# Layer 2's first product of blocks 1 to 4 by seven half-size products, with weights' sums formed during block 0

## The chip, the core and the metric

The kernel runs on one core of a Trainium2 chip. The core has a matrix engine (TensorE, PE in the profile; its weight loads are listed as PEld), a vector engine (VectorE, DVE), a scalar engine (ScalarE, ACT), GpSimd (POOL) and SyncE (SP), which here starts the transfers. Each engine works through its own list of instructions in order; semaphores make one engine wait for another. The matrix engine writes its results to PSUM, which has 8 banks; everything else that is kept on the core lies in SBUF, in tiles of 128 partitions.

The metric is the time of one execution in microseconds (us) on the device. The kernel before took 992.25 us, the median of 3 runs (991.37 to 992.49).

## What is computed

The reference is a causal attention with a memory term, followed by two layers with one hidden product each:

```python
x = attn_out.transpose(0, 2, 1, 3).reshape(B * S, H * D)    # 2304 tokens x 512
# layer 1: h = x @ w_in (512 x 2048); g = softplus(h); x = g @ w_out (2048 x 512)
# layer 2:
h = x @ w_in
r = np.maximum(h, 0.0)
g = r * r
return (g @ w_out).astype(np.float32)
```

B is 4, H is 8, S is 576, D is 64. The weights come as 64-bit floats and are turned into pairs on the core.

## The kernel before

Every matrix product works on pairs of 16-bit numbers: a value is kept as a high half and a low half (what the high half leaves over), and a product is three matmuls: high weights by high data, high weights by low data, low weights by high data (lines 708 to 710).

The kernel first runs attention and layer 1 interleaved, about 618 us of the span. Layer 1 works in 9 blocks of 256 tokens; each ends in `evac_x` (lines 472 to 475), where ScalarE writes the high half of the block's output (scaled by 2) and VectorE the low half (line 475). These halves are the input of layer 2, in tiles `x` of 512 tokens.

Layer 2 (lines 698 to 732) works in blocks of 512 tokens, four of them and a last one of 256, numbered 0 to 4. A block has two stages:

- The first product. For each of 16 chunks `f` of 128 hidden columns, 12 matmuls (4 chunks of the 512 inputs, 3 matmuls each) with 512 moving columns (256 in block 4) fill one PSUM bank `h2ps`. ScalarE applies Relu (712) into `r2` and squares it (713); VectorE makes the high half by a cast (715) and the low half by a subtraction (716). These go to `gg`, one pair of tiles for each `f`.
- The row tiles, one for each 128 tokens: 48 matmuls of 512 columns (724 to 726) sum over all 16 `f` into one bank `ops`; ScalarE copies it to `osb` (728) and SyncE sends it out (731).

`split_piece` (409 to 424) turns pieces of the 64-bit weights into pairs: VectorE has four instructions a piece (419, 420, 421, 424) and ScalarE one (423). Layer 2's 32 pieces go through it late in layer 1 and during block 0's first product: `W3` is w_in, `W4` is w_out.

The order of instructions on each engine is set when the program is built: a list scheduler places them by an estimate of its own, in the order of the code where priorities (`tc.high_priority`) don't say otherwise. The pools set when a tile's memory can be written again.

Of the kernel before, what the change touches and what calls it, by code (L numbers as in the profile page):

```python
# [31 lines left out]
LOE = 99  # L32
TQ = 2
TP = 2
GPL = 0
W34P = 0

KVB = 9
SPB = 2
# [9 lines left out]
def kernel(  # L49
# [15 lines left out]
    pe, act, dve, pool, sp = nc.tensor, nc.scalar, nc.vector, nc.gpsimd, nc.sync  # L65
# [3 lines left out]
    NCC = DM // P  # L69
# [291 lines left out]
    def x_at(kb):  # L361
        i, o = divmod(kb * NB, XB)
        return x_t[i][:, :, o:o + NB]
# [42 lines left out]
            )  # L406
        return t

    def split_piece(i, t, Ws, pool_, on_pool=False):
# [49 lines left out]
    def unit_x(kb, cp, f0=0, f1=NFC):  # L459
# [134 lines left out]
    def run_unit(u):  # L594
        if u[0] == "h":
            unit_h(u[1], u[2])
        elif u[0] == "x":
            unit_x(*u[1:])
        elif u[0] == "xq":
            unit_xq(u[1], u[2])  # L600
        elif u[0] == "close":
            close_start()
        else:
            i = u[1]
            with tc.high_priority(HW):
                split_piece(order[i], pieces.pop(i), (W1, W2), stage, on_pool=False)
# [66 lines left out]
    st2 = ctx.enter_context(st2_cm)  # L673
    nu = len(queue)
    pieces = {i: load_piece(i, (moe2_w_in, moe2_w_out), sp, st2) for i in range(ST2)}
    nxt = 0
# [18 lines left out]
    bp = ctx.enter_context(tc.tile_pool(name="bp", bufs=2, side="right", reuse_waits="tile"))  # L695
    mm2 = ctx.enter_context(tc.tile_pool(name="mm2", bufs=8, space=PSUM, reuse_waits="tile"))
    u2 = S_R / S_X2
    t0 = 0
    while t0 < NT:
        n = min(512, NT - t0)  # L700
        gs = []
        x = x_t[t0 // XB]
        for f in range(NFC):
            ps = mm2.tile([P, 512], F32, tag="mm2", name="h2ps")
            for c in range(NCC):
                wh, wl = (w[:, c, f * P:(f + 1) * P] for w in W3)
                xh, xl = (x[:, t * NCC + c] for t in range(2))
                pe.matmul(ps[:, :n], wh, xh, start=(c == 0), stop=False)  # L708
                pe.matmul(ps[:, :n], wh, xl, start=False, stop=False)  # L709
                pe.matmul(ps[:, :n], wl, xh, start=False, stop=(c == NCC - 1))  # L710
            r = bp.tile([P, 512], F32, name="r2", bufs=3)
            act.activation(r[:, :n], ps[:, :n], AF.Relu, scale=u2)  # L712
            act.activation(r[:, :n], r[:, :n], AF.Square)  # L713
            g = [bp.tile([P, 512], F16, name=f"gg{t}_{f}", bufs=1) for t in range(2)]
            dve.tensor_copy(g[0][:, :n], r[:, :n])  # L715
            dve.tensor_tensor(g[1][:, :n], r[:, :n], g[0][:, :n], ALU.subtract)
            gs.append(g)
            if t0 == 0:
                w34_to(NPC + f + 1)
        for m in range(n // P):  # L720
            ps = mm2.tile([P, 512], F32, tag="mm2", name="ops")
            for f in range(NFC):
                gh, gl = (t[:, m * P:(m + 1) * P] for t in gs[f])
                pe.matmul(ps, gh, W4[0][:, f, :], start=(f == 0), stop=False)  # L724
                pe.matmul(ps, gh, W4[1][:, f, :], start=False, stop=False)  # L725
                pe.matmul(ps, gl, W4[0][:, f, :], start=False, stop=(f == NFC - 1))  # L726
            o = bp.tile([P, 512], F32, name="osb", bufs=3)
            act.activation(o, ps, AF.Copy, scale=1.0 / (S_R * S_R))  # L728
            for b, s0, r0, k_ in segs(t0 // P + m):
                p0 = b * S + s0  # L730
                sp.dma_start(out=out[p0:p0 + k_, :], in_=o[r0:r0 + k_])
        t0 += n


# [27 lines left out]
```

## Time and profile before

| | |
|---|---|
| median of 3 runs | 992.25 us |
| the profiled execution, its own time | 997.09 us |
| its span, first to last instruction | 995.3 us |
| matmul busy | 907.6 us (91%) |
| VectorE busy | 584.9 us (59%) |
| ScalarE busy | 543.2 us (55%) |
| mean granted clock of TensorE | 0.984 of 2.4 GHz |

Busy times are sums of durations as the profiler reports them. A matmul's duration includes its way through the array, and matmuls overlap; the pace of a run of matmuls is read from the starts of its first and last one. A few per cent of the matmul records are missing from the trace, so counts of matmuls in a stretch are slightly low.

### The profile page before, as it was taken

The page shows a single profiled execution, that of the slowest core. Times are in us where ns is not written, and L with a number is a line of the kernel's source. Part 1 is how long each engine was busy: PE and PEld are TensorE (multiplying, and loading weights), DVE is VectorE, ACT ScalarE, POOL GpSimd, SP SyncE. Part 2 cuts the span into 40 slices and gives each one's busy share as a digit, 9 for nine tenths or more (in the row PEclk, how much of TensorE's full clock was granted, in tenths as well). Part 3 has the DMA queues.
Part 4 walks back from the last instruction along what each step waited for, and adds up shares of the span by engine and source line. Part 5 has one row for each costly group of instructions (what it writes and reads, how often), then busy time and mean ns, then how long its engine had stood idle before and what let it go on. Part 6 is the DMA issues. An engine that isn't in the chain of part 4 may idle for free.

```text
span 995.3 us, 20666 instructions
## 1 busy us (share of the span) xinstructions
PE 907.6 (91%) x8418; PEld 642.2 (65%) x8436; DVE 584.9 (59%) x1359; ACT 543.2 (55%) x1090; POOL 2.2 (0%) x10
## 2 busy tenths in 40 slices
PE   4336998899998999999999998999999999999998
PEld 3235787788887889888887886444444444444483
DVE  7998989868668676757755599950340141042040
ACT  8765868769669595958756384630340241142050
POOL 0000000000000000000000000000000000000000
PEclk9998999999999999999998999999999999999999
DMA  9999998775699955756743556500000000000000
GB/s 228 233 232 229 205 174 162 119 105 112 100 169 174 160 102 96 108 97 96 115 84 58 157 178 190 174 14 22 11 1 22 22 1 11 32 1 11 22 13 22
DMA packets 283216, 101.00 MB, mean 101 GB/s; under 512 B 248048, under 2 KB 280816, under 8 KB 283120
## 3 DMA queue, kind: packets, MB, share of 16 engines
q1 hardware_dynamic: 282880, 99.65, 50.5%
q8 instruction: 66, 1.08, 0.5%
q14 instruction: 30, 0.25, 0.1%
q10 hardware_dynamic: 240, 0.02, 0.0%
HBM read 48.78 MB, written 4.72 MB: 54 GB/s over the span
## 4 chain that ended last, share of the span: by engine, by line
PE 67%; DMA 14%; DVE 9%; ACT 5%; issue 3%; SPq 1%; ACTq 0%; DVEq 0%
PE ops L726 7%; DMA PT<-p 6%; PE h2ps L710 6%; PE h2ps L709 6%; PE h2ps L708 6%; PE ops L724 6%; PE ops L725 6%; PE xps L454 4%; PE xps L455 4%; PE xps L453 4%; PE s_ps L311 3%; PE hps L438 3%; PE hps L437 3%; PE hps L436 3%; PE pvt L356 3%
## 5 line engine op out<-in xcount | busy, mean ns | idle before, releaser
L715 DVE CAST gg<-r 128x512 f16<-128x512 f32 (+1 forms) x80 | 31.8, 398 | 238.0 <-ACT r L713 238.0
L436 PE MATMUL hps<-x,W 128*128 128x256 f16 x576 | 160.1, 278 | 3.5 <-DVE cc L275 2.1
L438 PE MATMUL hps<-x,W 128*128 128x256 f16 x576 | 160.0, 278 | 0.0
L437 PE MATMUL hps<-x,W 128*128 128x256 f16 x576 | 160.0, 278 | 0.0
L454 PE MATMUL xps<-g,W 128*128 128x256 f16 x512 | 139.7, 275 | 2.2 <-DVE g L447 2.2
L455 PE MATMUL xps<-g,W 128*128 128x256 f16 x512 | 140.0, 275 | 0.0
L453 PE MATMUL xps<-g,W 128*128 128x256 f16 x512 | 138.6, 275 | 1.3 <-DVE spa L443 0.7
L320 ACT ACTIVATE Pt<-Pt,cs 128x128 f32<-128x128 f32 (+4 forms) x144 | 84.1, 584 | 67.8 <-DVE cs L316 67.5
L311 PE MATMUL s_ps<-KT,qT 128*128 128x128 f16 (+2 forms) x992 | 83.8, 225 | 35.9 <-DVE cs L316 35.3
L708 PE MATMUL h2ps<-x,W 128*128 128x512 f16 (+1 forms) x320 | 114.5, 358 | 0.0
L709 PE MATMUL h2ps<-x,W 128*128 128x512 f16 (+1 forms) x320 | 114.5, 358 | 0.0
L710 PE MATMUL h2ps<-x,W 128*128 128x512 f16 (+1 forms) x320 | 114.5, 358 | 0.0
L726 PE MATMUL ops<-W,gg 128*128 128x512 f16 x288 | 109.2, 379 | 0.9
L724 PE MATMUL ops<-W,gg 128*128 128x512 f16 x288 | 109.2, 379 | 0.0
L728 ACT ACTIVATE osb<-ops 128x512 f32<-128x512 f32 x18 | 10.8, 597 | 172.8 <-PE ops L726 172.8
L725 PE MATMUL ops<-W,gg 128*128 128x512 bf16 x270 | 102.3, 379 | 0.0
L311 PEld LDWEIGHTS <-qT 128*128 128x128 f16 (+1 forms) x992 | 59.2, 105 | 47.7 <-issue 43.1
L333 DVE TENSOR_TENSOR p<-Pt,p 128x512 f16<-128x512 f32 (+2 forms) x104 | 69.5, 668 | 29.1 <-ACT p L332 28.4
L712 ACT ACTIVATE r<-h2ps 128x512 f32<-128x512 f32 (+1 forms) x80 | 44.2, 552 | 75.0 <-PE h2ps L710 75.0
L356 PE MATMUL pvt<-V,PT 128*128 128x64 f16 (+1 forms) x1392 | 62.1, 199 | 16.7 <-DMA PT<-p 15.6
L316 DVE CUSTOM_DVE_ANT_0 Pt<-s_ps,mask 128x128 f32<-128x128 f32 (+3 forms) x128 | 62.1, 485 | 17.3 <-PE s_ps L311 16.8
L332 ACT ACTIVATE p<-Pt 128x512 f16<-128x512 f32 (+2 forms) x104 | 62.9, 605 | 11.3 <-DMA PT<-p 10.3
(117 smaller groups left out, 1648.2 us busy)
## 6 DMA issues: line engine op xcount, KB each, us to landing
wst<-in_moe_w_in_dram SPq DMA_DIRECT2D x32, 512.0 KB, 5.0
wst<-in_moe_w_out_dram SPq DMA_DIRECT2D x32, 512.0 KB, 4.4
rawk<-in_k_dram SPq DMA_DIRECT2D x16, 256.0 KB, 4.1
rawq<-in_q_dram SPq DMA_DIRECT2D x16, 256.0 KB, 3.5
rawv<-in_v_dram SPq DMA_DIRECT2D x16, 256.0 KB, 4.1
out_dram<-osb SPq DMA_DIRECT2D x16, 256.0 KB, 2.0
PT<-p SPq DMA_TRANSPOSE x100, 3.4
mraw<-in_M_prev_dram SPq DMA_DIRECT2D x8, 128.0 KB, 3.8
```

The source lines that it names most:

```text
L311: pe.matmul(o[x * n:(x + 1) * n], qT[g][:, t * H + h, x * n:(x + 1) * n], KT[kb][:, h, a - j * P:e - j * P], start=(t == 0), stop=(t == 1),)
L436: pe.matmul(o, wh, x[:, c], start=(c == 0), stop=False)
L437: pe.matmul(o, wh, x[:, NCC + c], start=False, stop=False)
L438: pe.matmul(o, wl, x[:, c], start=False, stop=(c == NCC - 1))
L453: pe.matmul(ps, wh, gh, start=(f == f0), stop=False)
L454: pe.matmul(ps, wh, gl, start=False, stop=False)
L455: pe.matmul(ps, wl, gh, start=False, stop=(f == f1 - 1))
L708: pe.matmul(ps[:, :n], wh, xh, start=(c == 0), stop=False)
L709: pe.matmul(ps[:, :n], wh, xl, start=False, stop=False)
L710: pe.matmul(ps[:, :n], wl, xh, start=False, stop=(c == NCC - 1))
L724: pe.matmul(ps, gh, W4[0][:, f, :], start=(f == 0), stop=False)
L726: pe.matmul(ps, gl, W4[0][:, f, :], start=False, stop=(f == NFC - 1))
```

## The change

Blocks 1 to 4 of layer 2 form their first product in another way. The 512 inputs are cut into two halves, the 2048 hidden columns into two halves, and a block's tokens into two halves. A product of 2 x 2 such parts takes eight part products; by Strassen's method (in Winograd's form) it takes seven, of sums and differences of the parts:

- `sums_w` forms four sums of weight parts, `WS`, in four calls, each with ten VectorE additions of 512 columns into an fp32 tile `T`, one ScalarE cast and one VectorE subtraction of 2048 columns. They stand in the code behind block 0's first product.
- `x_parts` forms the seven input operands of a block, `XT`: three of the parts themselves and four sums. It reads the input in fp32; so `evac_x` no longer splits the output of layer 1 for its blocks 2 to 8 but writes it once, in fp32, into the same memory (`x2_at`).
- `seven_h(j, n)` does two hidden chunks of each half (four of the 16 `f`) at a time: seven products of 12 matmuls with 256 columns (128 in block 4), each into one bank; ScalarE copies the first to SBUF, VectorE adds the others in seven instructions (P1 to P7 below are in the order of the code), and `finish` does Relu, Square, the cast (now on ScalarE) and the subtraction on 1024 columns at once, for each half of the hidden columns.
- Block 0 keeps the plain product (`plain_h`), with the chunks in another order; the tiles `gg` are now four pairs, one for each `j`, and `row_tile` sums over the chunks in the order of `j`.
- The pool of 64-bit pieces is closed behind block 0's first product, and the pool of `WS`, `XT` and `T` is opened there. Some unused switches go.

```diff
@@ -469 +467 @@
+    def x2_at(kb):
+        i, o = divmod(kb * NB, XB)
+        return x_t[i].bitcast(F32)[:, :, o // 2:(o + NB) // 2]
+
     def evac_x(kb, c, ps):
+        if kb * NB >= XB:
+            o = x2_at(kb)[:, 2 * c.start:2 * c.stop]
+            act.activation(o, ps.rearrange("p c (j t) -> p (c j) t", j=2), AF.Copy, scale=S_X2)
+            return
         hi, lo = (x_at(kb)[:, t * NCC:(t + 1) * NCC][:, c] for t in range(2))
...
@@ -695 +701 @@
+    HF = NFC // 2
...
+    def finish(r, hi, lo):
+        act.activation(r, r, AF.Relu, scale=u2)
+        act.activation(r, r, AF.Square)
+        act.activation(hi, r, AF.Copy)
+        dve.tensor_tensor(lo, r, hi, ALU.subtract)
...
+    def sums_w(k, c0):
+        c1 = slice(c0, c0 + 512)
+        c2 = slice(DFF // 2 + c0, DFF // 2 + c0 + 512)
+        (h11, l11), (h21, l21), (h12, l12), (h22, l22) = [
+            [w[:, k + d, c] for w in W3] for d, c in ((0, c1), (0, c2), (2, c1), (2, c2))
+        ]
+        T = sp2.tile([P, 4, 512], F32, name="T", bufs=1)
+        s1, s2, s3, s4 = (T[:, i] for i in range(4))
+        dve.tensor_tensor(s1, h21, h22, ALU.add)
+        dve.tensor_tensor(s3, h11, h21, ALU.subtract)
+        dve.tensor_tensor(s1, s1, l21, ALU.add)
...
+        dve.tensor_tensor(s4, s4, l12, ALU.add)
+        hi, lo = (w[:, :, k, c1] for w in WS)
+        act.activation(hi, T, AF.Copy)
+        dve.tensor_tensor(lo, T, hi, ALU.subtract)
+
+    def x_parts(t0):
...
+        (b11, b12), (b21, b22) = q
+        T = sp2.tile([P, 4, 512], F32, name="T", bufs=1)
+        t1, t2, t3, t4 = (T[:, i, :n].rearrange("p (a t) -> p a t", a=a) for i in range(4))
+        dve.tensor_tensor(t1, b12, b11, ALU.subtract)
+        dve.tensor_tensor(t3, b22, b12, ALU.subtract)
+        dve.tensor_tensor(t2, b22, t1, ALU.subtract)
+        dve.tensor_tensor(t4, b21, t2, ALU.subtract)
+        for i, y in enumerate((b11, b21, b22)):
+            hi, lo = (z[:, i, :n].rearrange("p (a t) -> p a t", a=a) for z in XT)
+            act.activation(hi, y, AF.Copy)
+            dve.tensor_tensor(lo, y, hi, ALU.subtract)
+        act.activation(XT[0][:, 3:, :n], T[:, :, :n], AF.Copy)
+        dve.tensor_tensor(XT[1][:, 3:, :n], T[:, :, :n], XT[0][:, 3:, :n], ALU.subtract)
...
+    def seven_h(j, n):
+        hn = n // 2
+
+        def prod(w, x):
+            ps = mm2.tile([P, 512], F32, tag="mm2", name="h2ps")[:, :n]
+            for i in range(2):
+                o = ps[:, i * hn:(i + 1) * hn]
+                for k in range(2):
+                    wh, wl = w3_at(w, k, j + i)
+                    xh, xl = (y[:, x, k * hn:(k + 1) * hn] for y in XT)
+                    pe.matmul(o, wh, xh, start=(k == 0), stop=False)
+                    pe.matmul(o, wh, xl, start=False, stop=False)
+                    pe.matmul(o, wl, xh, start=False, stop=(k == 1))
+            return ps
+
+        r = [bp.tile([P, 2, 512], F32, name="r2", bufs=4) for _ in range(2)]
+        (r11, r12), (r21, r22) = [[y[:, i, :n] for i in range(2)] for y in r]
+        new_g(j)
+        act.activation(r11, prod(0, 0), AF.Copy)
+        dve.tensor_tensor(r12, prod(4, 4), r11, ALU.add)
+        dve.tensor_tensor(r22, prod(5, 5), r12, ALU.add)
+        dve.tensor_tensor(r21, prod(2, 6), r22, ALU.add)
+        p5 = prod(3, 3)
+        dve.tensor_tensor(r22, p5, r22, ALU.add)
+        dve.tensor_tensor(r12, p5, r12, ALU.add)
+        for h in (1, 0):
+            if h == 0:
+                dve.tensor_tensor(r11, prod(1, 1), r11, ALU.add)
+                dve.tensor_tensor(r12, prod(6, 2), r12, ALU.add)
+            finish(*(z[:, :, :n] for z in (r[h], gg[j][0][:, h], gg[j][1][:, h])))
+
+    def row_tile(t0, m, hn):
...
+        fs = [(j, i, h) for j in range(0, HF, 2) for i in range(2) for h in range(2)]
+        for a, (j, i, h) in enumerate(fs):
...
-    t0 = 0
-    while t0 < NT:
...
-        for f in range(NFC):
...
+    for j in range(0, HF, 2):
+        plain_h(j)
+        w34_to(NPC + 2 * j + 4)
+    st2_cm.__exit__(None, None, None)
+    sp2 = ctx.enter_context(tc.tile_pool(name="sums", bufs=1, reuse_waits="tile"))
+    WS = [sp2.tile([P, 4, 2, DFF // 2], t, name=f"WS{i}") for i, t in enumerate((F16, BF16))]
+    XT = [sp2.tile([P, 7, 512], F16, name=f"XT{t}") for t in range(2)]
+    x_parts(XB)
+    for c0 in (0, 512):
+        for k in range(2):
+            sums_w(k, c0)
+    for m in range(XB // P):
+        row_tile(0, m, XB // 2)
+    for t0 in range(XB, NT, XB):
+        n = min(XB, NT - t0)
+        for j in range(0, HF, 2):
+            seven_h(j, n)
+        if t0 + n < NT:
+            x_parts(t0 + n)
         for m in range(n // P):
...
+            row_tile(t0, m, n // 2)
```

The first place is TensorE's list at the start of block 1's first product. `x1` is the input tile of that block, `W30` and `W31` the halves of w_in, `XT0` and `XT1` the halves of the operands. Before, and then now:

```order
L708 MATMUL h2ps_10468<-x1_62,W30_9098 128x512
L709 LDWEIGHTS W30_9098
L709 MATMUL h2ps_10468<-x1_62,W30_9098 128x512
L710 LDWEIGHTS W31_9099
L710 MATMUL h2ps_10468<-x1_62,W31_9099 128x512
L708 LDWEIGHTS W30_9098
```

```order
L799 MATMUL h2ps_10507<-XT0_10228,W30_9087 128x256
L800 LDWEIGHTS W30_9087
L800 MATMUL h2ps_10507<-XT1_10229,W30_9087 128x256
L801 LDWEIGHTS W31_9088
L801 MATMUL h2ps_10507<-XT0_10228,W31_9088 128x256
L799 LDWEIGHTS W30_9087
L799 MATMUL h2ps_10507<-XT0_10228,W30_9087 128x256
```

Each matmul has its own weight load in both; a matmul now has 256 columns and reads `XT`, and 336 of them stand where 192 stood (in block 4, 336 of 128 columns for 192 of 256).

The second place is VectorE's list behind block 0's last `gg`. Before, the next block's `gg` follows at once; now, the end of `x_parts` and the sums come first. Before, and then now:

```order
L716 TENSOR_TENSOR gg1_14_10225<-r2_10221,gg0_14_10224 128x512
L715 CAST gg0_15_10250<-r2_10247 128x512
L716 TENSOR_TENSOR gg1_15_10251<-r2_10247,gg0_15_10250 128x512
L715 CAST gg0_0_10484<-r2_10481 128x512
L716 TENSOR_TENSOR gg1_0_10485<-r2_10481,gg0_0_10484 128x512
```

```order
L736 CAST gg0_6_10124<-r2_10193 128x2x256
L775 TENSOR_TENSOR T_10230<-x1_62,T_10230 128x512
L737 TENSOR_TENSOR gg1_6_10125<-r2_10193,gg0_6_10124 128x2x256
L781 TENSOR_TENSOR XT1_10229<-T_10230,XT0_10228 128x2048
L747 TENSOR_TENSOR T_10243<-W30_9087 128x512
L748 TENSOR_TENSOR T_10243<-W30_9087 128x512
L749 TENSOR_TENSOR T_10243<-T_10243,W31_9088 128x512
L750 TENSOR_TENSOR T_10243<-T_10243,W31_9088 128x512
```

Between block 0's last subtraction and block 1's first addition there now stand one subtraction of `x_parts` and the sums of `sums_w`; the fourth call's last seven instructions stand among the additions of block 1.

The third place is TensorE's list in block 1's row tiles, behind 12 matmuls of `gg` 0, 12 of `gg` 2 and 2 of `gg` 4 of the first tile, 12 of `gg` 0 of the second tile, 10 of `gg` 4 and the first 4 of `gg` 2 (the numbers behind `gg0_` and `gg1_` are `j`, and the halves 0 high and 1 low; `ops` tells the tile):

```order
L828 LDWEIGHTS gg0_2_10616
L828 MATMUL ops_11012<-W41_9090,gg0_2_10616 128x512
L829 LDWEIGHTS gg1_2_10617
L829 MATMUL ops_11012<-W40_9089,gg1_2_10617 128x512
L827 LDWEIGHTS gg0_6_10838
L827 MATMUL ops_10960<-W40_9089,gg0_6_10838 128x512
L828 LDWEIGHTS gg0_6_10838
L828 MATMUL ops_10960<-W41_9090,gg0_6_10838 128x512
L827 LDWEIGHTS gg0_2_10616
L827 MATMUL ops_11012<-W40_9089,gg0_2_10616 128x512
```

Before, a row tile's list ran straight over the 16 chunks; now the chunks of `gg` 6, which are finished last, are put behind the start of the second tile, and 54 matmuls stand before the first of them. The last of ScalarE's list for block 1's first product, for the same place:

```order
L712 ACTIVATE r2_10725<-r2_10725 128x1024
L714 ACTIVATE gg0_4_10727<-r2_10726 128x1024
L713 ACTIVATE r2_10725<-r2_10725 128x1024
L780 ACTIVATE XT0_10228<-T_10947 128x2048
L714 ACTIVATE gg0_4_10727<-r2_10725 128x1024
L778 ACTIVATE XT0_10228<-x2_2699 128x512
L712 ACTIVATE r2_10837<-r2_10837 128x1024
L778 ACTIVATE XT0_10228<-x2_2699 128x512
```

The casts and the copies of the next block's `XT` stand among the last `finish`; `XT0` is written there once the products that read it are done.

## Rows read from the trace of the kernel before

**Rows 1.** Page, part 1: busy us, share of the span, instructions, by engine.
```profile
PE 907.6 (91%) x8418; PEld 642.2 (65%) x8436; DVE 584.9 (59%) x1359; ACT 543.2 (55%) x1090; POOL 2.2 (0%) x10
```

**Rows 2.** Busy time by stage: stretch, length, busy (instructions) of each engine, clock, DMA.
```profile
core 0: us, PE busy (x) PEld busy (x) DVE busy (x) ACT busy (x) POOL busy (x), PEclk, DMA share, GB/s
...
273.00:570.00 297.00, 285.07 (x3670) 250.19 (x3671) 198.62 (x493) 204.33 (x432) 0.00 (x0) 0.99 0.67 117
570.00:604.00 34.00, 31.47 (x286) 27.76 (x284) 33.90 (x62) 26.25 (x45) 0.00 (x0) 1.00 0.60 182
604.00:617.80 13.80, 13.53 (x108) 11.40 (x108) 12.82 (x24) 3.38 (x7) 0.00 (x0) 0.88 0.63 196
617.80:659.30 41.50, 41.50 (x194) 18.79 (x193) 40.93 (x80) 25.73 (x45) 0.00 (x0) 1.00 0.41 127
659.30:701.50 42.20, 41.99 (x194) 19.13 (x196) 2.56 (x5) 3.68 (x7) 0.00 (x0) 1.00 0.05 19
701.50:742.50 41.00, 40.95 (x191) 18.59 (x191) 16.80 (x30) 18.89 (x31) 0.00 (x0) 1.00 0.02 7
950.00:971.00 21.00, 20.95 (x189) 18.39 (x188) 10.79 (x30) 12.80 (x32) 0.00 (x0) 1.00 0.04 14
971.00:995.30 24.30, 19.81 (x92) 8.82 (x90) 0.72 (x2) 1.21 (x3) 0.00 (x0) 0.97 0.08 23
```

**Rows 3.** Chain of waits from 618 us to the end, by line.
```profile
by line: PE ops L726 17.3%; PE h2ps L710 16.5%; PE h2ps L709 16.5%; PE ops L724 16.5%; PE h2ps L708 16.4%; PE ops L725 15.5%; issue 0.3%; ACT osb L728 0.2%
```

**Rows 4.** Timeline of ScalarE: start us, duration, instruction, [idle before, releaser].
```profile
669.50 0.60 ACT L728 ACTIVATE osb<-ops 128x512 f32<-128x512 f32 x1 [8.88 <-PE ops L726]
679.86 0.60 ACT L728 ACTIVATE osb<-ops 128x512 f32<-128x512 f32 x1 [9.76 <-PE ops L726]
```

**Rows 5.** Timeline of TensorE: first and last of 24 consecutive 256-column matmuls.
```profile
169.74 0.27 PE L436 MATMUL hps<-x,W 128*128 128x256 f16 x1
...
172.25 0.27 PE L438 MATMUL hps<-x,W 128*128 128x256 f16 x1
```

**Rows 6.** Timeline of TensorE: six 128-column matmuls, and what follows them.
```profile
174.60 0.50 PE L311 MATMUL s_ps<-KT,qT 128*128 128x128 f16 x6
174.94 0.27 PE L454 MATMUL xps<-g,W 128*128 128x256 f16 x1
```

**Rows 7.** Groups by line and shape from 640 us on: count, busy us, mean ns, idle.
```profile
L716 DVE TENSOR_TENSOR gg<-r,gg 128x512 f16<-128x512 f32 x58 | 40.0, 690 | 5.1
L713 ACT ACTIVATE r<-r 128x512 f32<-128x512 f32 x56 | 35.3, 630 | 1.7
L712 ACT ACTIVATE r<-h2ps 128x512 f32<-128x512 f32 x56 | 33.3, 595 | 66.9 <-PE h2ps L710 66.9
...
L716 DVE TENSOR_TENSOR gg<-r,gg 128x256 f16<-128x256 f32 x16 | 6.8, 426 | 1.7
L713 ACT ACTIVATE r<-r 128x256 f32<-128x256 f32 x16 | 6.7, 417 | 0.5
```

**Rows 8.** Timeline of VectorE at the end of block 0's first product.
```profile
656.39 0.68 DVE L716 TENSOR_TENSOR gg<-r,gg 128x512 f16<-128x512 f32 x1
656.99 0.68 DVE L421 SCALAR_TENSOR_TENSOR wcv<-wst,wcv 128x512 int32<-128x512 int32 x1
...
658.53 0.68 DVE L424 TENSOR_TENSOR W<-wcv,W 128x512 bf16<-128x512 f32 x1
...
661.24 0.69 DVE L716 TENSOR_TENSOR gg<-r,gg 128x512 f16<-128x512 f32 x1
```

**Rows 9.** Line 475, all its instructions: count, ns shortest/median/longest, first and last start.
```profile
L475 DVE SCALAR_TENSOR_TENSOR x<-xps,x x14: 682/686/693, 273.2 to 618.3; 128x512 f16<-128x512 f32 x14
```

**Rows 10.** Groups of VectorE from 570 to 604 us, line 475 alone.
```profile
L475 DVE SCALAR_TENSOR_TENSOR x<-xps,x 128x512 f16<-128x512 f32 x1 | 0.7, 682 | 0.0
```

**Rows 11.** Timeline of TensorE behind its last wait of layer 1.
```profile
604.27 0.27 PE L454 MATMUL xps<-g,W 128*128 128x256 f16 x1 [1.36 <-DVE g L447]
...
604.95 0.42 PE L453 MATMUL xps<-g,W 128*128 128x256 f16 x1
605.16 0.42 PE L454 MATMUL xps<-g,W 128*128 128x256 f16 x1
```

More of the change, by code (lines that the diff above doesn't have):

```diff
@@ L34 @@
 TP = 2
-GPL = 0
-W34P = 0
 KVB = 9
@@ L407, in load_piece, with split_piece @@
         return t
-    def split_piece(i, t, Ws, pool_, on_pool=False):
+    def split_piece(i, t, Ws, pool_):
         W = Ws[i // NPC]
@@ L605, in run_unit @@
             with tc.high_priority(HW):
-                split_piece(order[i], pieces.pop(i), (W1, W2), stage, on_pool=False)
+                split_piece(order[i], pieces.pop(i), (W1, W2), stage)
             if i + NST < 2 * NPC:
@@ L672 @@
     st2_cm = tc.tile_pool(name="st2", bufs=ST2, reuse_waits="tile")
-    st2 = ctx.enter_context(st2_cm)
+    st2 = st2_cm.__enter__()
     nu = len(queue)
@@ L680, in w34_to @@
         while nxt < m:
-            split_piece(nxt, pieces.pop(nxt), (W3, W4), st2, on_pool=nxt % 4 < W34P)
+            split_piece(nxt, pieces.pop(nxt), (W3, W4), st2)
             if nxt + ST2 < 2 * NPC:
@@ L697 @@
     u2 = S_R / S_X2
-    t0 = 0
-    while t0 < NT:
-        n = min(512, NT - t0)
-        gs = []
-        x = x_t[t0 // XB]
-        for f in range(NFC):
[L704 to L719, printed above, removed]
-        for m in range(n // P):
[L721 to L732, printed above, removed]
@@ new lines, with new_g, plain_h @@
+    HF = NFC // 2
+    gg = {}
+    def new_g(j):
+        gg[j] = [bp.tile([P, 2, 2, 512], F16, name=f"gg{t}_{j}", bufs=1) for t in range(2)]
+        return gg[j]
+    def finish(r, hi, lo):
[3 more added lines that the diff above has]
+        dve.tensor_tensor(lo, r, hi, ALU.subtract)
+    def plain_h(j):
+        x = x_t[0]
+        new_g(j)
+        for h in range(2):
+            for i in range(2):
+                f = h * HF + j + i
+                ps = mm2.tile([P, 512], F32, tag="mm2", name="h2ps")
+                for c in range(NCC):
+                    wh, wl = (w[:, c, f * P:(f + 1) * P] for w in W3)
+                    xh, xl = (x[:, t * NCC + c] for t in range(2))
+                    pe.matmul(ps, wh, xh, start=(c == 0), stop=False)
+                    pe.matmul(ps, wh, xl, start=False, stop=False)
+                    pe.matmul(ps, wl, xh, start=False, stop=(c == NCC - 1))
+                r = bp.tile([P, 2, 512], F32, name="r2", bufs=4)[:, 0]
+                act.activation(r, ps, AF.Relu, scale=u2)
+                act.activation(r, r, AF.Square)
+                hi, lo = (g[:, h, :, i * 256:(i + 1) * 256] for g in gg[j])
+                r = r.rearrange("p (a t) -> p a t", a=2)
+                dve.tensor_copy(hi, r)
+                dve.tensor_tensor(lo, r, hi, ALU.subtract)
@@ new lines, in x_parts @@
+    def x_parts(t0):
+        n = min(512, NT - t0)
+        if n == 512:
+            q = [[x2_at(t0 // NB + t)[:, 4 * d:4 * d + 4] for t in range(2)] for d in range(2)]
+            a = 4
+        else:
+            q = [[x2_at(t0 // NB)[:, 4 * d + t:4 * d + 4:2] for t in range(2)] for d in range(2)]
+            a = 2
+        (b11, b12), (b21, b22) = q
[11 more added lines that the diff above has]
+        dve.tensor_tensor(XT[1][:, 3:, :n], T[:, :, :n], XT[0][:, 3:, :n], ALU.subtract)
@@ new lines, in w3_at @@
+    def w3_at(w, k, f):
+        if w < 3:
+            o, c = ((0, 0), (0, 2), (DFF // 2, 2))[w]
+            return [y[:, c + k, o + f * P:o + (f + 1) * P] for y in W3]
+        return [y[:, w - 3, k, f * P:(f + 1) * P] for y in WS]
+    def seven_h(j, n):
+        hn = n // 2
+        def prod(w, x):
+            ps = mm2.tile([P, 512], F32, tag="mm2", name="h2ps")[:, :n]
+            for i in range(2):
+                o = ps[:, i * hn:(i + 1) * hn]
[8 more added lines that the diff above has]
+        (r11, r12), (r21, r22) = [[y[:, i, :n] for i in range(2)] for y in r]
+        new_g(j)
+        act.activation(r11, prod(0, 0), AF.Copy)
[10 more added lines that the diff above has]
+            finish(*(z[:, :, :n] for z in (r[h], gg[j][0][:, h], gg[j][1][:, h])))
@@ new lines, in row_tile @@
+    def row_tile(t0, m, hn):
+        ps = mm2.tile([P, 512], F32, tag="mm2", name="ops")
+        th, o = divmod(m * P, hn)
+        fs = [(j, i, h) for j in range(0, HF, 2) for i in range(2) for h in range(2)]
+        for a, (j, i, h) in enumerate(fs):
+            f = h * HF + j + i
+            gh, gl = (g[:, h, th, o + i * hn:o + i * hn + P] for g in gg[j])
+            pe.matmul(ps, gh, W4[0][:, f, :], start=(a == 0), stop=False)
+            pe.matmul(ps, gh, W4[1][:, f, :], start=False, stop=False)
+            pe.matmul(ps, gl, W4[0][:, f, :], start=False, stop=(a == NFC - 1))
+        o = bp.tile([P, 512], F32, name="osb", bufs=3)
+        act.activation(o, ps, AF.Copy, scale=1.0 / (S_R * S_R))
+        for b, s0, r0, k_ in segs(t0 // P + m):
+            p0 = b * S + s0
+            sp.dma_start(out=out[p0:p0 + k_, :], in_=o[r0:r0 + k_])
```

10 lines of the change are left out of this document (8 added, 2 removed).

## The prediction

> **What bounds the kernel now.** I read the page's busy shares first: matmuls 91% of the span, VectorE 59%, ScalarE 55% [rows 1]. Then the table by stage, because the change sits in one part only. From 617.80 us on, TensorE is busy without a gap in every stretch (41.50 of 41.50 us, 41.99 of 42.20) at a clock of 1.00, which is 2.4 GHz, while VectorE has 2.56 us of work in a row stage and 16.80 us in a first product of 41.00 us [rows 2]. The chain of waits says the same: behind 618 us, over 98% of it is the six matmul lines [rows 3]. So in layer 2 a matmul column taken away shortens the run, as long as the engines that empty PSUM keep up. Block 0's first product is the exception: there VectorE is busy 40.93 of 41.50 us with weight pieces [rows 2]. Before 617.80 the bound is mixed; between 570 and 604 us it is VectorE (33.90 of 34.00) [rows 2].
>
> **Pace of the matmuls.** A row tile is 48 matmuls of 512 columns, and two `osb` copies that wait for it start 669.50 and 679.86: 10.36 us, 0.2158 us each [rows 4]. 24 matmuls of 256 columns start from 169.74 to 172.25: 23 steps, 0.1091 us [rows 5]. Six of 128 columns take 174.60 to 174.94: 0.0567 us, each with its own weight load [rows 6].
>
> **What goes, on TensorE.** Before, a first product of blocks 1 to 3 is 192 x 0.2158 = 41.4 us. Now it is 4 steps of `j` x 7 products x 12 matmuls = 336 of 256 columns, 36.7 us: 4.8 us less, 14.3 us over three blocks. Block 4: 192 x 0.1091 = 20.9 us before (the stretch shows 20.95 [rows 2]), 336 x 0.0567 = 19.0 us now: 1.9 us less. Together 16.2 us. Row tiles and block 0 keep their matmuls.
>
> The 128-column pace rests on short runs inside other work, so I bound it. Below, half the 256-column step, 0.0546: 0.7 us better. Above, a weight load's own duration, were loads not to overlap: 18.39 us for 188 of them in block 4 before, 0.098 us [rows 2], by which block 4 would take 32.9 us, 13.9 us more than with the pace I take. That is 0.0567, since its row has matmuls of this width, each with a load.
>
> **What comes in, on VectorE and ScalarE.** ScalarE takes 630 ns for 512 columns and 417 for 256; VectorE 690 and 426 [rows 7]. The wide operations have no row; in a line from these two widths, 1024 columns are 1.06 us on ScalarE and 1.22 on VectorE, 2048 are 1.91 and 2.27. Lower bound: VectorE's starts are 0.60 us apart where a duration says 0.68 [rows 8], so the sums below are some 10% high; upper bound: twice the 512-column duration, 1.26 and 1.38 for 1024.
>
> - A step of `j`: ScalarE 0.60 + 6 x 1.06 = 7.0 us, VectorE 7 x 0.69 + 2 x 1.22 = 7.3 us, beside 12 x 7 x 0.1091 = 9.2 us of matmuls. By the upper bound it is 8.2 and 7.6: still under. In block 4, 0.42 + 6 x 0.63 = 4.2 and 7 x 0.43 + 2 x 0.69 = 4.4 us, beside 4.8: narrow, but 8 banks stand between, and a delay in the middle of the block is made up. I price it 0, bound 2 us.
> - `x_parts`: VectorE 7 x 0.69 + 2.27 = 7.1, ScalarE 3 x 0.63 + 1.91 = 3.8 us a block. Its operands for the next block may be written only when the last step's products have read the old ones, so it falls on the end of a stage. A block's VectorE work is then 4 x 7.3 + 7.1 = 36.3 beside 36.7 us of matmuls, and what is late goes on into the row stage, where VectorE had 2.56 us to do in 42 [rows 2].
> - The end of a stage is the place to watch. I counted along the changed order with these durations from the start of block 1. ScalarE's last cast of `gg` 6 ends 9.2 us after the last product, VectorE's last subtraction 10.5. TensorE has 54 matmuls of 0.2158 = 11.7 us to do before it asks for `gg` 6, and 24 (5.2 us) before `gg` 4, whose last cast ends at 1.7. In block 2 the same count gives 7.2 and 8.4 us. So nothing is late, by 1 to 4 us. I price 0.5 us in all, bound 9 us (3 us a block).
> - The sums: one call is 10 x 0.69 + 1.91 + 2.27 = 11.1 us, as the tile `T` is single and the casts alternate with VectorE. VectorE is through with block 0's last subtraction at about 661.9 us [rows 8]; `x_parts` adds some 4 us to that, so the calls start near 666 and end near 677, 688, 699 and, interleaved with block 1's additions, 717. Block 1 starts near 617.8 + 2 x 41.4 = 700.6; its steps 0 and 2 need the first two calls, step 4 the last two from 700.6 + 18.3 + 1.3 = 720.2. Row tiles, which need no VectorE, are the cover; without it all 44 us would be on the path. I price 0, bound 3 us.
> - The last `gg` of block 0 comes some 2 us later (three subtractions of `x_parts` in front). TensorE asks for it after 36 matmuls of the row tile, 7.8 us: 0.
> - SyncE's transfers are the same in number; the weights' pieces of layer 2 come at the same rate, and the new pools lie on memory whose readers are done by then.
>
> **Before layer 2.** 14 VectorE instructions of 0.69 us go (line 475, from 273.2 us on) [rows 9], 9.6 us of VectorE time, of which only one lies in the stretch that VectorE bounds [rows 10]: 0.6 us gained. But the scheduler's order of attention and layer 1 differs from the first of them on. TensorE is busy 285.07 of 297 us between 273 and 570 [rows 2], so no order can win more than some 12 us there, and a likely one moves a few us either way. I take 0, bound -4 to +5.
>
> **The sum.** 16.2 + 0.6 - 0.5 = 16.3 us less. The profiled execution took 997.09 us (span 995.3 and 1.8 around it), so it would take 980.8; the median of the runs shown is 4.8 us lower, 992.25, and the forecast is 992.25 - 16.3 = 975.9 us, say 976.
>
> **The rivals.**
>
> - The first 618 us come out differently. For it: the order there changes; TensorE has waits of up to 1.36 us there [rows 11]. Against: the same work, little idle time to win. 971 or 982.
> - The stage ends stall. If the wide casts take 20% more than my line, `gg` 6 is late in block 1. I price a wait of 3 us in each of three blocks, and the clock: behind the last wait of layer 1, 1.36 us, matmuls of 256 columns ran 0.21 us apart, half pace, 1.2 GHz [rows 11], and the stretch from 604.00 to 617.80 has a mean clock of 0.88 [rows 2], which is 1.7 us lost. 3 x (3 + 1.7) = 14.1: 990 us, faster by 0.2%.
> - The weight loads hold the 128-column matmuls, at 0.098 us each: 13.9 us more, 990. For it: 336 in a row is a longer run than any of this width before. Against: six of them at 0.0567 with their loads [rows 6]. The Trainium skill, "TensorE: Matmul & The Clock Gate", section "Back-to-back issue gap", says that a real stream of weight loads and matmuls sustains 81 ns at 128 columns and 131 ns at 512. By that block 4 would be 27.2 us and the time 984; the trace does not agree, with 57 ns at 128 columns [rows 6] and 216 at 512 [rows 4].
> - Slower: the emptying of PSUM becomes the bound of `seven_h`. Place: the chain product 1, copy on ScalarE, four additions on VectorE each on the one before, then Relu, Square, cast, subtraction. If the two engines only took turns, a step would be 7.0 + 7.3 = 14.3 us, 12 steps 172 us for 124 before, block 4 8.6 x 4 = 34 for 21: 1053 us. It decides from 41.4 / 4 = 10.4 us a step on. For it: the chain is long and ScalarE's order is fixed. Against: two pairs of `r2` and 8 banks let two steps overlap, and each engine alone has 7 of 9.2 us.
> - That the matmuls don't fall to seven eighths: the order shows 336 for 192 at half the columns, so only the pace could undo it.
>
> **Chances.** The forecast, 972 to 980: 0.68. The first part better (under 972) 0.07, worse (980 to 985) 0.10. Stage ends 0.06. Weight loads 0.03. PSUM emptying 0.06, half of it so mild that the kernel stays faster. A measurement of this kernel tells a change from none at about 0.2%, 2 us. Faster by more than that: 0.85 of the first three, 0.05 of the stage ends, 0.02 of the weight loads and 0.03 of the emptying, 0.95; within it 0.02; slower 0.03. The range 969 to 984 leaves out about 0.03 below and 0.15 above.
>
> **What would show it.** In the profile after: first products of blocks 1 to 3 of 36.7 us and of block 4 of 19, TensorE busy without gaps over the four row stages, clock 1.00 there; VectorE's sums ending before 720 us and no TensorE wait on `WS`; ScalarE and VectorE at 70 to 90% in first products; start of block 0 near 617.8. I am wrong if TensorE shows waits on `gg` at the start of row tiles or on PSUM in `seven_h`, or if layer 2 starts more than 5 us from 617.8.

## The result: 13.9 us faster, and the profile after

The changed kernel takes 977.92 us, the median of 4 runs (977.57 to 981.02), against 991.81 us (989.22 to 992.49) for the kernel before on the same chip: a ratio of 0.9872 (0.9845 to 0.9899). The forecast was 976.0. The profiled execution took 977.68 us, its span 975.9.

The page's busy times, for [rows 1]: TensorE has 576 matmuls more and 23.4 us less to do, VectorE 83 and ScalarE 44 us more.
```profile
PE 884.2 (91%) x8994; PEld 680.1 (70%) x9012; DVE 668.0 (68%) x1437; ACT 587.2 (60%) x1094; POOL 2.2 (0%) x10
```
Busy time by stage, for the part of [rows 2] behind 617.80 (the same columns). The stretches are block 0's first product and row tiles, then block 1's and 2's, and the last block's first product:
```profile
614.50:656.00 41.50, 41.50 (x195) 18.83 (x194) 41.40 (x82) 26.21 (x45) 0.00 (x0) 1.00 0.44 137
656.00:697.60 41.60, 41.39 (x191) 18.93 (x194) 33.88 (x46) 12.11 (x12) 0.00 (x0) 1.00 0.05 20
697.60:734.30 36.70, 36.70 (x337) 32.80 (x336) 34.92 (x50) 24.47 (x26) 0.00 (x0) 1.00 0.02 8
734.30:775.70 41.40, 41.19 (x190) 18.83 (x193) 9.62 (x11) 9.07 (x12) 0.00 (x0) 1.00 0.05 20
775.70:812.40 36.70, 36.70 (x337) 32.82 (x336) 24.96 (x34) 24.14 (x27) 0.00 (x0) 1.00 0.02 8
...
931.90:950.90 19.00, 19.00 (x338) 18.84 (x337) 13.64 (x33) 13.34 (x25) 0.00 (x0) 1.00 0.05 16
```
The third row is the change: 336 matmuls in 36.70 us, where the product took 41.4. TensorE is full in each first product and its clock 1.00 in every row. The second row holds the sums: 33.88 us of VectorE work where there had been 2.56. What they leave over stands in the third, where VectorE is at 95%, and is gone in the fifth, at 68%.

The chain of waits from 614.5 us to the end, by line, for [rows 3]: the row tiles' matmuls (827 to 829), those of the seven products (799 to 801) and block 0's (728 to 730). No other engine has a share that counts.
```profile
by line: PE ops L829 18.0%; PE ops L827 17.2%; PE ops L828 16.1%; PE h2ps L801 11.9%; PE h2ps L799 11.9%; PE h2ps L800 11.9%; PE h2ps L730 3.8%; PE h2ps L729 3.8%; PE h2ps L728 3.8%; issue 0.3%; ACT osb L831 0.2%; PE xps L452 0.0%; PE xps L
```
The last `osb` copies of blocks 0 to 3, in ScalarE's timeline, give the time of a block:
```profile
697.67 0.60 ACT L831 ACTIVATE osb<-ops 128x512 f32<-128x512 f32 x1 [1.41 <-PE ops L829]
...
775.79 0.60 ACT L831 ACTIVATE osb<-ops 128x512 f32<-128x512 f32 x1 [9.81 <-PE ops L829]
...
853.91 0.60 ACT L831 ACTIVATE osb<-ops 128x512 f32<-128x512 f32 x1 [9.81 <-PE ops L829]
...
932.03 0.60 ACT L831 ACTIVATE osb<-ops 128x512 f32<-128x512 f32 x1 [9.81 <-PE ops L829]
```
They are 78.12 us apart. Before, the same copies were 82.88 apart, all three times; of the first two and of the very last copy, ScalarE's timeline has:
```profile
700.63 0.60 ACT L728 ACTIVATE osb<-ops 128x512 f32<-128x512 f32 x1 [9.81 <-PE ops L726]
...
783.51 0.60 ACT L728 ACTIVATE osb<-ops 128x512 f32<-128x512 f32 x1 [9.81 <-PE ops L726]
...
990.90 0.60 ACT L728 ACTIVATE osb<-ops 128x512 f32<-128x512 f32 x1 [9.76 <-PE ops L726]
```
The step is 4.76 us shorter, three times, 14.3 us. From block 0's first matmul of layer 2 to the very last copy it is 373.4 us before (617.5 to 990.90) and 357.0 after (614.5 to 971.46): layer 2 gives 16.4 us, and the last block's part of that is 2.2.

Layer 2's start moved too, from 617.5 to 614.5 us in these two profiles. That is no gain to count: a second profile of the kernel before starts layer 2 at 609.1 us and a second one of the changed kernel at 617.7. The next section looks at the first part by itself.

### The profile page after: what moved, and what is told of

It is laid out like the page before. It is cut to its first block, busy times and chain, and to the rows that moved or that the text cites. A ratio compares the mean times of both kernels' runs of the same rounds, so it can differ in the third digit from the quotient of the medians.

```text
span 975.9 us, 21791 instructions
## 1 busy us (share of the span) xinstructions
PE 884.2 (91%) x8994; PEld 680.1 (70%) x9012; DVE 668.0 (68%) x1437; ACT 587.2 (60%) x1094; POOL 2.2 (0%) x10
## 4 chain that ended last, share of the span: by engine, by line
PE 60%; DMA 16%; DVE 13%; ACT 6%; issue 3%; SPq 1%; ACTq 0%; DVEq 0%
DMA PT<-p 8%; PE ops L829 7%; PE ops L827 6%; PE ops L828 6%; PE h2ps L801 4%; PE h2ps L799 4%; PE h2ps L800 4%; DMA rawq<-in_q_dram 3%; PE xps L452 3%; PE xps L451 3%; PE xps L453 3%; PE s_ps L309 3%; PE pvt L354 2%; PE hps L436 2%; PE hps L435 2%
## 5 line engine op out<-in xcount | busy, mean ns | idle before, releaser
L434 PE MATMUL hps<-x,W 128*128 128x256 f16 x576 | 157.8, 276 | 3.2 <-DVE cc L273 3.0
L435 PE MATMUL hps<-x,W 128*128 128x256 f16 x576 | 158.4, 276 | 1.7 <-ACT x L477 1.7
L436 PE MATMUL hps<-x,W 128*128 128x256 f16 x576 | 158.2, 275 | 0.0
L831 ACT ACTIVATE osb<-ops 128x512 f32<-128x512 f32 x18 | 10.8, 597 | 123.4 <-PE ops L829 123.4
L808 DVE TENSOR_TENSOR r<-h2ps,r 128x512 f32<-128x512 f32 (+1 forms) x16 | 10.0, 623 | 108.0 <-PE h2ps L801 107.2
L354 PE MATMUL pvt<-V,PT 128*128 128x64 f16 (+1 forms) x1392 | 60.7, 197 | 19.5 <-DMA PT<-p 18.3
L354 PEld LDWEIGHTS <-PT 128*128 128x128 f16 (+1 forms) x1392 | 50.3, 104 | 28.7 <-DMA PT<-p 25.1
L435 PEld LDWEIGHTS <-W 128*128 128x128 f16 x576 | 56.9, 99 | 10.2 <-issue 3.6
L799 PE MATMUL h2ps<-XT,WS 128*128 128x256 f16 (+1 forms) x256 | 63.7, 259 | 0.0
L800 PE MATMUL h2ps<-XT,WS 128*128 128x256 f16 (+1 forms) x256 | 63.7, 259 | 0.0
```

Of the source, the lines that this page charges most:

```text
L354: pe.matmul(o[r], t[:, o0 + i + y, r], V[kb][:, z, h, :], start=(i == 0 and y + z == 0), stop=(i == nb - 1 and y > 0),)
L799: pe.matmul(o, wh, xh, start=(k == 0), stop=False)
```

## The experiments

The first three ask about layer 2: what holds its 16.4 us, and how close it is to losing them. The others ask about the first 618 us.

**A row tile must be through before the next begins.** After the change, block 1's first two tiles end at 750.49 and 755.02, 4.5 us apart, where a tile is 10.4 us of matmuls: the scheduler begins the second before the first is done. This kernel forbids that; `q0` is a tile's first matmul, `q1` its last:
```diff
+    last = []
...
+            if a == 0 and last:
+                tc.add_manual_dep(
+                    q0.ins, last[0].ins.name,
+                    mybir.DependencyInfo(mybir.DependencyClass.NoSync, mybir.DependencyReason.DATA),
+                    reason="tile order",
+                )
...
+        last[:] = [q1]
```


> The row tiles are kept one behind the other in TensorE's order, so gg 6 is asked for after 36 matmuls (7.8 us) and not after 54. My count of the stage end (last cast 9.2 us, last subtraction 10.5 us behind the last product of block 1; 7.2 and 8.4 in block 2): TensorE waits some 2.3 us in block 1 and 0.2 in blocks 2 and 3, 2.5 to 3 us more in all, and up to 1.7 more if its clock falls. Rival: the durations are a little short as counted, nothing is late, 0.

Measured: 983.22 us, ratio 0.99 (0.9868 to 0.9931) to the kernel before, which took 994.62 us on the chip of this run and the next two. Its blocks 1, 2 and 3 take 79.81, 78.56 and 78.12 us: 1.69, 0.44 and 0 more. TensorE's waits behind 620 us in this kernel (what was waited for, us in total, times, longest):
```profile
PE ops L837 <- DVE gg L715: 1.8, 2, 1.5
```
Both are for VectorE's half of `gg`. The longer one in TensorE's timeline, some 10 us after block 1's last product:
```profile
748.80 0.39 PE L837 MATMUL ops<-W,gg 128*128 128x512 f16 x1 [1.52 <-DVE gg L715]
```
So a tile in its own order does come to `gg` 6 before VectorE has it, worst in block 1, where the sums' remainder stands in front. What covers the subtraction is the next tile's matmuls, put in between. The margin is there, and it is thin.

**One call of the sums too many.** `sums_w` is called five times, the first of them twice over:
```diff
     x_parts(XB)
+    sums_w(0, 0)
     for c0 in (0, 512):
```


> One of the four calls that form the weights' sums runs twice (10.8 us more of VectorE in block 0's row stage). If the row stage covers the sums with only the 2 us to spare that the profile after shows (the last sums are there at 714.9, TensorE asks for them at 717.2), the kernel is 8.5 us slower or more, as the additions of block 1 stand in between: 986 to 993. Rival: VectorE has room enough in block 1 to catch up, under 3 us.

Measured: 990.86 us, ratio 0.9964 (0.9942 to 0.9986); block 1 takes 87.18 us, 9.06 more, and the other blocks none. TensorE's one wait, in its timeline:
```profile
734.12 0.40 PE L799 MATMUL h2ps<-XT,WS 128*128 128x256 f16 x1 [7.31 <-ACT WS L758]
```
and its stretch by stage:
```profile
701.60:747.00 45.40, 38.08 (x335) 33.05 (x334) 41.80 (x59) 23.84 (x25) 0.00 (x0) 0.92 0.02 7
```
7.3 us are the wait; the other 1.7 go with the clock, 0.92 over the stretch: the matmul behind the wait lasts 0.40 us, where 0.27 is usual. The last of the casts that write `WS`, in ScalarE's timeline of the changed kernel and then of this one:
```profile
710.49 1.90 ACT L758 ACTIVATE WS<-T 128x2048 f16<-128x2048 f32 x1
```
```profile
732.16 1.91 ACT L758 ACTIVATE WS<-T 128x2048 f16<-128x2048 f32 x1 [2.97 <-DVE T L756]
```
It ends 14.7 us into block 1 in the changed kernel and 32.4 us into it here. That is 17.7 us later for an added call of 10.8, because VectorE's work on block 1 stands between the additions of the last call. But TensorE covered more than the margin: it came to the wait 25.2 us into the block, some 5.6 us later than it first needs the last two calls in the changed kernel, as the scheduler had put matmuls that need no late sum in front. The four calls cost nothing because block 0's row tiles leave VectorE 39 us, not because they are small.

**Two buffers of `r2` for four**, which is one pair for a step of `j`:
```diff
-        r = [bp.tile([P, 2, 512], F32, name="r2", bufs=4) for _ in range(2)]
+        r = [bp.tile([P, 2, 512], F32, name="r2", bufs=2) for _ in range(2)]
```
(and the same in `plain_h`).


> The sums of the products have one pair of r2 tiles and not two, so a step of j can't begin its additions before the step in front is through Relu, Square, cast and subtraction. Rival 'PSUM emptying' of the prediction: the two engines take turns and a step costs up to 14.3 us for 9.2, 1040 to 1050 us in all. If the 8 banks of PSUM alone carry it: 977.9 to 985.

Measured: 983.71 us, ratio 0.9903 (0.9865 to 0.9941). Only block 1 is longer, 80.19 us, by 2.07. TensorE's one wait:
```profile
732.77 0.27 PE L799 MATMUL h2ps<-XT,WS 128*128 128x256 f16 x1 [1.73 <-ACT r L807]
```
With one pair, a step's emptying begins only when the last one's is done, and it falls behind. Block 2's last subtraction, in VectorE's timeline of this kernel and then of the changed one:
```profile
833.21 1.23 DVE L715 TENSOR_TENSOR gg<-r,gg 128x1024 f16<-128x1024 f32 x1 [0.81 <-ACT gg L714]
```
```profile
819.58 1.22 DVE L715 TENSOR_TENSOR gg<-r,gg 128x1024 f16<-128x1024 f32 x1
```
It ends 15.5 us behind the block's first product here (which is done at 818.9) and 8.6 us behind it in the changed kernel (812.2). Blocks 2 and 3 lose nothing even so, because the order gives more cover: the first row tile ends 22.2 us behind the product (copy at 841.13), where the changed kernel has 15.1 (827.31), so more matmuls of the other tiles stand in front of `gg` 6. Block 1 is the exception, perhaps because VectorE has the sums to finish there; no run separates the two.

**The first part alone.** The kernel before with `evac_x`'s fp32 write and nothing else of the change; ahead of the row tiles the two halves that layer 2 needs are made again (a cast on ScalarE, a subtraction on VectorE), and all first products keep their 192 matmuls:
```diff
+        if kb * NB >= XB:
+            o = x2_at(kb)[:, 2 * c.start:2 * c.stop]
+            act.activation(o, ps.rearrange("p c (j t) -> p (c j) t", j=2), AF.Copy, scale=S_X2)
+            return
```


> The other half alone: layer 1's output is written once in fp32, with the changed kernel's order of the first 618 us, and layer 2 keeps its 192 plain matmuls a block; the halves are made in the row stage before (ScalarE 2 x 1.06, VectorE 2 x 1.22 us a block, hidden). Theory A: 991.8 + 2.6 = 994.4 us. Rival B: 991.8. Rival C: 988.8.

**The products alone.** The changed kernel with `evac_x` as before: `x_parts` first adds the two halves again, into a tile `F`:
```diff
-        if kb * NB >= XB:
-            o = x2_at(kb)[:, 2 * c.start:2 * c.stop]
-            act.activation(o, ps.rearrange("p c (j t) -> p (c j) t", j=2), AF.Copy, scale=S_X2)
-            return
...
+        F = sp2.tile([P, 4, 512], F32, name="F", bufs=1)
...
+                dve.tensor_tensor(q[d][t], y[:, 2 * d:2 * d + 2], y[:, NCC + 2 * d:NCC + 2 * d + 2], ALU.add)
```


> Layer 1's output is split into halves as in the kernel before, so that the order of the first 618 us is that of before; x_parts adds the halves back together (4 more VectorE additions a block), and blocks 1 to 4 use the seven products. Theory A (the seven products save 16.5 us in layer 2, as the profile after shows, and the new order of the first part gives some 2.6 of it back in the median): 991.8 - 16.5 = 975.3 us, 2.6 under the changed kernel. Rival B (the first part is as fast in either order, and layer 2 saves 13.9 in the runs that aren't profiled): 977.9, as the changed kernel. Rival C (the new order saves 3 us, as the two profiles read side by side say): 979 to 981, slower than the changed kernel.

Beside these two ran the changed kernel and the kernel before once more.


> The changed kernel again, for the comparison on one chip: 977.9 us by all theories, 13.9 under the kernel before.

> The kernel before again, for a second profile. Theory A and rival B: its first part ends at 612 to 614 us in this one, for the first profile (997.1 us) was 4.8 us longer than the median and layer 2 has nothing that could vary. Rival C: 617.5 again.

Measured on one chip, the kernel before at 992.49 us (17 runs): the first part alone 996.65, ratio 1.0035 (1.0018 to 1.0052); the products alone 978.63, ratio 0.9861 (0.9841 to 0.9881); the changed kernel 980.53, ratio 0.9876 (0.9858 to 0.9895). The single run of the kernel before gave 988.7.

In the profiles layer 2 takes 373.4 us in the first part alone and 357.0 in the products alone, the same as in before and after (the last two columns of the table below). So all of the gain is the products', and the fp32 write costs: 3.5 us by the timed runs (0.0035 x 992.49, interval 1.8 to 5.2), all of it ahead of layer 2. Gain and cost together make 12.9 us, and after's three comparisons show 13.9, 12.0 and 15.8.

Where that cost sits is seen in ScalarE's copies of layer 1's output. In the first part alone TensorE's instructions of attention and layer 1 stand in the same order as in after; in the products alone they stand as in before. Starts in us of the second copy of block 2, the first of block 3, the second of block 7, the first matmul of layer 2 and the last `osb` copy, in each profile:
```
                 block 2   block 3   block 7   layer 2   last copy
before            287.98    335.75    570.84    617.5      990.90
before_again      284.77    333.75    563.93    609.1      982.52
pairs_seven       287.02    335.12    570.53    617.3      974.26
pairs_seven2      291.89    340.46    571.26    616.0      972.88
fp32_from7        290.59    338.80    570.37    614.7      971.62
after             287.64    343.69    570.30    614.5      971.46
after_again       286.87    345.30    573.34    617.7      974.58
after_third       286.08    345.25    572.27    616.3      973.23
fp32_only         287.90    345.63    574.55    618.6      992.02
```
The two rows `pairs_seven` and `pairs_seven2` are the products alone, `fp32_from7` is the last experiment. With the old order, block 3's first copy comes 48 to 49 us behind block 2's second; with the new one 56 to 59. That is 7 to 11 us later, with no overlap between the two groups. Most of it is made up again: to block 7's second copy it is 279 to 284 us by the old order, 283 to 287 by the new. From there to layer 2 the new order is the quicker: 44 us, where the old one has 45 to 47. VectorE, which bounds that stretch [rows 2], has less to do there; with the old order and that relief (`fp32_from7`) it is 44 too.

TensorE's waits from 286 to 570 us, the kernel before:
```profile
PE pvt L356 <- DMA PT<-p: 9.7, 14, 1.4
PE hps L436 <- DMA x<-xn: 1.1, 1, 1.1
...
```
Transfers of `PT` make most of it, 9.7 of 11.8 us. The same in the first part alone:
```profile
PE pvt L356 <- DMA PT<-p: 12.8, 14, 2.5
PE hps L437 <- ACT x L479: 2.0, 1, 2.0
PE s_ps L311 <- DVE cs L316: 1.5, 3, 0.7
```
Here it is 16.3 us. And in the changed kernel:
```profile
PE pvt L354 <- DMA PT<-p: 11.7, 13, 2.3
PE hps L435 <- ACT x L477: 1.7, 1, 1.7
PE s_ps L309 <- DVE cs L314: 1.2, 3, 0.7
```
It is 14.6 us there. The second line of the last two fences is new: a matmul of layer 1 waits for the fp32 write (line 479 or 477). TensorE's timeline in the changed kernel's second run:
```profile
287.50 0.27 PE L435 MATMUL hps<-x,W 128*128 128x256 f16 x1 [1.57 <-ACT x L477]
```
and ScalarE's at the same time:
```profile
286.87 0.58 ACT L477 ACTIVATE x<-xps 128x512 f32<-128x512 f32 x1
```
The matmul starts as that write, of block 2's output, ends. A tile of `x` holds two blocks, and block 3's input is in the same tile as block 2's output, at other columns. That the program orders the one behind the other for the tile's sake is what the row suggests; it was not tried with a tile of its own. With the longer waits for `PT`, TensorE waits 4.5 us more than in the kernel before in the first part alone, and 2.8 in the changed kernel.

The other profiles fall in the same two groups. Between block 2's second copy and block 7's, TensorE waits 9.8 to 11.8 us in the five with the old order and 14.6 to 16.3 in the four with the new one, in each of them most of it for `PT`. The means are 4.8 us apart, and the stretch itself is 4.6 us longer in the mean. So the stretch grows by what TensorE waits more; that block 3's copy comes later costs nothing in itself, as TensorE does other work meanwhile. The quicker stretch behind block 7's copy gives 1.7 us back in the mean, which leaves some 3 us, near the 3.5 of the timed runs. Why the transfers of `PT` are waited for longer in the new order is open.

**The fp32 write in blocks 7 and 8 alone**, late enough to leave the scheduler's order of the first blocks as it was and to relieve VectorE where it is the bound. For the other blocks `x_parts` adds the halves into `F`, as in the products alone. In `evac_x`:
```diff
-        if kb * NB >= XB:
+        if kb >= 7:
```
It ran beside the products alone and the changed kernel.


> Only the last two blocks of layer 1 (7 and 8) are kept as fp32, the others are split as before and x_parts adds their halves up; TensorE's order of the first 618 us is word for word that of before, and four VectorE instructions are missing, all behind 560 us. Theory A (the new order costs some 4 us between 288 and 570 us in TensorE's waits, and the relief of VectorE behind 570 gives 2.6 back): both kernels are beaten, 992.5 - 16.4 - 2.6 = 973.5 us, 5 to 7 under the changed kernel. Rival B (what the first part takes scatters from run to run, and the order is not the cause): 978 to 980, as the changed kernel.

> Layer 1's output all in halves and before's order, seven products, a second time beside the others. Theory A: 992.5 - 16.4 = 976.1 us. Rival B: 978 to 980.

> The changed kernel, a third time beside the others. Theory A: 979 to 980.5 us, 3 or 4 above the kernel with before's order and 6 above the one with fp32 from block 7. Rival B: no difference beyond the scatter.

Measured on one chip, the kernel before at 993.61 us (11 runs): 974.98 us (973.8 to 977.8), ratio 0.9804 (0.9776 to 0.9831), for blocks 7 and 8 alone; 978.9, ratio 0.984 (0.981 to 0.9869), for the products alone; 977.83, ratio 0.9836 (0.9808 to 0.9864), for the changed kernel. Layer 2 is 356.9 us in all three profiles. The first is the quickest kernel here, some 3 us under the changed kernel by medians; the two intervals overlap.

The products alone do not fit this account. They have the order of before and layer 2's whole gain, so they should have been some 2 to 4 us quicker than the changed kernel, and were 1.9 us quicker on one chip and 1.1 slower on the other. By the ratios' intervals (an estimate) these two differences are uncertain by some 3 and 4 us, so they neither show a loss of 3 us nor exclude it. That the new order costs 3.5 us in the plain kernel is measured; that the changed kernel loses as much to it is not shown. The closest comparison is that of the changed kernel with the one that has the fp32 write in blocks 7 and 8 alone, where layer 2 and the stretch behind block 7 are equal and the order differs: 2.9 us by medians, and four of its five runs lie under all five of the changed kernel's. VectorE's relief in blocks 7 and 8, which the products alone lack and which is worth one to two us in the profiles, may make up part of it. Single profiles can't settle the rest: the kernel before itself began layer 2 at 617.5 and at 609.1 us.

## Why the prediction was right, step by step

**The main term was right to a fifth of a microsecond.** 16.2 us were forecast from TensorE's columns; layer 2 is 16.4 us shorter. Blocks 1 to 3 gave 3 x 4.76 = 14.3, as worked out. Block 4 gave 2.2 for 1.9. The first and last matmul around block 4's first product:
```profile
931.78 0.22 PE L799 MATMUL h2ps<-XT,W 128*128 128x128 f16 x1
...
950.54 0.38 PE L827 MATMUL ops<-W,gg 128*128 128x512 f16 x1
```
18.76 us for 336 matmuls are 55.8 ns each, for 56.7 taken from a run of six [rows 6]. The rival that weight loads hold them at 98 ns is out. The Trainium skill, "TensorE: Matmul & The Clock Gate", section "Back-to-back issue gap", has 81 ns for a sustained stream at 128 columns; the trace does not agree, as 336 in a row, each with its own load, kept 56.

**The wide operations were on the line.** Groups by line and shape from 697 us on, for [rows 7] (count, busy us, mean ns, idle before):
```profile
L715 DVE TENSOR_TENSOR gg<-r,gg 128x1024 f16<-128x1024 f32 x24 | 29.3, 1222 | 10.6 <-ACT gg L714 10.5
L714 ACT ACTIVATE gg<-r 128x1024 f16<-128x1024 f32 x24 | 25.3, 1055 | 0.5
...
L759 DVE TENSOR_TENSOR WS<-T,WS 128x2048 bf16<-128x2048 f32 x2 | 4.6, 2288 | 2.0 <-ACT WS L758 2.0
L781 DVE TENSOR_TENSOR XT<-T,XT 128x2048 f16<-128x2048 f32 x2 | 4.6, 2283 | 0.0
L780 ACT ACTIVATE XT<-T 128x2048 f16<-128x2048 f32 x2 | 3.8, 1908 | 0.8 <-PE h2ps L801 0.8
```
Forecast were 1.22 and 1.06 us for 1024 columns and 2.27 and 1.91 for 2048. A straight line through two widths was enough.

**The emptying of PSUM: 0, as priced.** No wait of TensorE's behind 620 us, in any block. VectorE stood at 68% and ScalarE at 66% of a first product (24.96 and 24.14 of 36.70 in block 2), a little under the 70 to 90 expected; 95% for VectorE in block 1 with the sums. So the slower rival, by which the two engines only take turns at 14.3 us a step, is out for two pairs of `r2`. Its limit of 10.4 us a step is too strict: with one pair, block 2's last two steps came 11.1 and 15.8 us apart (their last subtractions start at 806.25, 817.38 and 833.21), and the block was no longer for it, since it has only four steps and the row stage takes up what is late.

**The sums: 0, as priced, with less room than it looks.** The last `WS` write in VectorE's timeline:
```profile
712.63 2.28 DVE L759 TENSOR_TENSOR WS<-T,WS 128x2048 bf16<-128x2048 f32 x1
```
It ends at 714.9. By the count of the forecast the step that reads it comes 18.3 + 1.3 us into block 1, here 697.6 + 19.6 = 717.2: 2.3 us to spare, for 3 forecast. A call took 10.8 us for 11.1. The fifth call showed what lies behind this margin: 9.06 us on the path, the lost clock included.

**The stage ends: 0 for 0.5.** The last cast and the last subtraction of block 1, each from its engine's timeline; the product ended at 734.1:
```profile
740.55 1.06 ACT L714 ACTIVATE gg<-r 128x1024 f16<-128x1024 f32 x1
...
742.70 1.22 DVE L715 TENSOR_TENSOR gg<-r,gg 128x1024 f16<-128x1024 f32 x1
```
ScalarE is through 7.5 us after the product, for 9.2 forecast, VectorE 9.8 for 10.5; TensorE asks after 54 matmuls, at 11.7. The margin that the changed order gives was counted rightly, and the tile-by-tile kernel shows what it is worth: 2.1 us over two blocks, not 9.

**The term that was mis-sized is "before layer 2".** It was priced at 0.6 us gained, with bounds of -4 and +5. The runs point to a loss: the fp32 write by itself measured 3.5 us of it (1.8 to 5.2), and the gains of 13.9, 12.0 and 15.8 us are 2.5, 4.4 and 0.6 short of layer 2's 16.4. The second sign is weak by itself, for the products alone, with the old order, were 2.5 and 1.7 short too; that part stays open. The step that failed is that the order's change was taken as even in sign. It had a direction: with the fp32 write, block 3's output comes 7 to 11 us later, some 2 us of it behind a wait that was not there before, and up to block 7 TensorE waits 4.8 us more in the mean of the profiles. The 0.6 us of VectorE's stretch was sound in kind: that stretch did get shorter, by 1.7 us in the mean. As the changed program starts layer 2 at 614.5 to 617.7 us and the old one at 609.1 and 617.5, the forecast of 617.8 within 5 us held. A gain of 16.3 us was forecast and 13.9 measured (10.0 to 15.4): layer 2 gave 0.7 more (16.4 for 16.2 - 0.5), the part ahead of it lost 2.5 where 0.6 was to be gained, and the two errors partly cancel.

## What to carry to other kernels

Where one engine is busy without a gap in a stage, price a change there by that engine's columns at the pace of its own rows, then ask of each added operation what it lies beside and when its result is first read: that gave 16.2 us for 16.4. Work is free only as far as its cover goes, so count the margin in microseconds (2.3 us here) and expect a lost clock on top once it is gone. An edit that stores a value in another form can also change the order and the waits far from it, here by 3.5 us; look for that in the stages ahead of the one you mean to change, and run that edit alone.

## What the runs showed of the hardware

TensorE's granted clock in the first 100 us was 0.62 of 2.4 GHz in the mean in the profile after, where the profile before had 0.97, at the same busy time. The stretch in the changed kernel:
```profile
0.00:100.00 100.00, 46.15 (x488) 35.68 (x489) 86.06 (x238) 68.41 (x152) 2.24 (x10) 0.62 1.11 230
```
and in the kernel before:
```profile
0.00:100.00 100.00, 46.11 (x486) 35.59 (x487) 86.34 (x238) 68.48 (x152) 2.23 (x10) 0.97 1.12 231
```
Nothing came later for it: block 2's second copy stands at 287.64 us after and at 287.98 before. In that stretch TensorE is busy under half the time, and VectorE 86 of the 100 us.

The first part of one program scatters: two profiles of the kernel before begin layer 2 at 617.5 and 609.1 us, and all of the 8.4 us lies ahead of it, since layer 2 takes 373.4 in both. From there on profiles of one program agree to 0.1 us. A change to layer 2 is measured better by the span of layer 2 than by the time of the run.
